# More dummy products of ones in jobs 1 and 2 of a one-core attention and feed-forward kernel

## Chip, cores, metric

The kernel runs on one core of a Trainium2 chip. The metric is the time of one execution on the device in microseconds; of several executions the median is taken. A core has five engines that run their own instruction streams side by side: PE (TensorE, matrix products; its weight loads are shown apart as PEld), DVE (VectorE), ACT (ScalarE), POOL (GpSimd) and SP (SyncE, which here issues the transfers). Each engine works through its own stream in a fixed order, and waits on semaphores that other engines and transfers raise.

## What is computed

Causal attention with a bias for 4 batches of 8 heads (576 positions, 64 columns per head), then two feed-forward layers on the joined heads. Cut to what matters:

```python
def _attn_ref(q, k, v, s):
    scores = scale * np.matmul(q, k.transpose(0, 1, 3, 2))
    cum = np.cumsum(np.maximum(s, 0.0), axis=-1)
    bias = -(cum[:, :, :, None] - cum[:, :, None, :])
    scores = np.where(causal, -1000000000.0, scores + np.minimum(bias, 0.0))
    attn = np.exp(scores - np.max(scores, axis=-1, keepdims=True))
    attn = attn / (np.sum(attn, axis=-1, keepdims=True) + 1e-09)
    return np.matmul(attn, v)
def _moe_ref(x, mu_k, mu_r, w_k, w_v, w_r):   # x_prev is x shifted by one position
    xk = mu_k * x + (1.0 - mu_k) * x_prev
    xr = mu_r * x + (1.0 - mu_r) * x_prev
    k = np.maximum(xk @ w_k, 0.0)
    return sigmoid(xr @ w_r) * (k * k @ w_v)
# a second feed-forward layer (_moe2_ref) with a norm and a gate over positions follows
```

The change touches nothing of this: it adds products whose results are never read.

## The kernel before, in words

Attention is cut into jobs, one job a pair of heads and some blocks of rows. For the first batch each pair makes two jobs: jobs 0 to 3 hold the row blocks 0, 1 and 2 of the four pairs, jobs 4 to 7 the blocks 3 and 4. A job of the first four has five score steps. A score step (`scores`, lines 366 to 411) is a product of queries and keys into a PSUM bank (line 366, full float32), a fold with the mask and the row minimum on DVE (line 381), an exponential on ACT (line 408), and then some **dummy products**: a 128 x 384 product of bfloat16 ones into the bank named `warm` (line 411), whose result nobody reads. How many stand behind each score step of job n is `WD[n]` (line 42), and jobs from the fifth on have none. Each dummy is tied by `behind` to the score product just issued: a tie of order alone, without a semaphore. In `rows` a job turns its probabilities with PE transposes (line 445) into two banks, ACT copies a bank (line 449), and products with the values follow (lines 451 and 455). Behind the transposes of a bank stand `WT[n]` dummies (lines 447 and 448). The first block of rows has its own small chain: line 463 on POOL, a transpose (465), a copy on ACT (467), products (471) and copies (472), and the job ends with a transpose (483) and a copy on ACT (484).

While jobs 0 to 7 run, weights come in. SP issues the loads of queries, keys, the bias row and values of the coming jobs (`load`, lines 203 to 220) and of the weights' words (`load_words`, line 100), all on one queue, in one order; `fetch` calls for the operands of the next job or two, which can only be written once the job before the last has read its own. Each piece of a weight is then taken apart by ACT and DVE (`assemble` and `convert`, lines 111 to 115, 72 and 75): the first step of each conversion is an ACT instruction (line 111) that needs the words to have landed. ACT runs these between the exponentials and copies of the jobs, in its one order.

`step(att, PA)` and `step(cvs, PC)` give the instructions of attention and of the conversions their priorities (-1000 and -500, a lower figure first), and the planner puts every engine's stream into a fixed order ahead of the run by a timeline of its own (`schedule_with_timeline_sim=True`). PE starts with 22 dummies (line 264) while the first operands are loaded. From about 60 us on the first feed-forward layer (line 690) runs beside the attention of the later jobs, then the second layer. The bank `warm` comes out of the pool of two banks that the feed-forward products use; it is given up after the last dummy of job 3.

```python
WD = (2, 1, 1, 2)
WT = (2, 1)
...
            for _ in range(WD[w.n] if w.n < len(WD) else 0):
                behind(nc.tensor.matmul(idle[:, 0:384], ones[:, 0:P], ones, start=True, stop=True), issued[0])
...
            for _ in range(WT[w.n] if w.n < len(WT) else 0):
                behind(nc.tensor.matmul(idle[:, 0:384], ones[:, 0:P], ones, start=True, stop=True), issued[0])
            nc.scalar.copy(tiles[tag][:, o : o + 512], bank)
```

Of the kernel before, what the change touches and what calls it, by code (L numbers as in the profile page):

```python
# [38 lines left out]
NS, NV = 8, 8  # L39
PACE = 3  # L40

WD = (2, 1, 1, 2)
WT = (2, 1)
GT = 150
N0 = 8
ENG0 = {"qh": "DA", "ql": "P", "kh": "A", "kl": "D", "vh": "DA", "vl": "P"}
# [7 lines left out]
def block_kernel(ctx: ExitStack, tc: tile.TileContext, qkv, vb, s, w_r, w_k, w_v, mu, w_in, w_out, w_sgT, g_ln, b_sg, out):  # L54
# [105 lines left out]
    def behind(i, j):  # L160

        kind = mybir.DependencyInfo(mybir.DependencyClass.NoSync, mybir.DependencyReason.DATA)
        tc.add_manual_dep(i.ins, j.ins.name, kind)
# [207 lines left out]
    def scores(w):  # L371
# [13 lines left out]
        for j, i in w.steps[0] + w.steps[1]:  # L385
# [23 lines left out]
            exps.append(i)  # L409
            for _ in range(WD[w.n] if w.n < len(WD) else 0):  # L410
                behind(nc.tensor.matmul(idle[:, 0:384], ones[:, 0:P], ones, start=True, stop=True), issued[0])
# [8 lines left out]
    def rows(w):  # L420
# [15 lines left out]
        for tag, o, pieces, ready in plan:  # L436
# [3 lines left out]
            for x, (i, j, c) in enumerate(pieces):  # L440
# [5 lines left out]
                at[i, j, c] = tiles[tag][:, o + x * P : o + (x + 1) * P]  # L446
            for _ in range(WT[w.n] if w.n < len(WT) else 0):
                behind(nc.tensor.matmul(idle[:, 0:384], ones[:, 0:P], ones, start=True, stop=True), issued[0])
# [749 lines left out]
```

## Time and profile before

| what | value |
|---|---|
| median of 3 runs | 676.12 us (674.73 to 676.29) |
| the profiled execution's own time | 676.66 us |
| its span, first to last instruction | 674.8 us |
| outside the span | 1.86 us |
| PE busy | 653.7 us, 97% of the span |
| DVE, ACT, POOL busy | 519.8, 426.1, 46.2 us |
| mean granted clock of TensorE | 0.997 of full speed |

The profile is that of one execution, 0.54 us above the median of the runs. The span is what the trace covers. Times in the trace count from its start, in microseconds. A PE row's duration includes the drain of the last product, so two rows that follow each other closely overlap by a fraction of a microsecond; the distance of their starts is what PE spent. What follows "idle before" names the engine, tile and line that ended a wait.

### The profile page before, as it was taken

What the parts mean: (1) busy time and instruction counts of PE and PEld (TensorE: products, weight loads), DVE (VectorE), ACT (ScalarE), POOL (GpSimd) and SP (SyncE); (2) the same over time, 40 slices, a digit from 0 to 9 for tenths busy, and PEclk for the clock granted to TensorE, in tenths of its full rate; (3) what the DMA queues carried; (4) which work ended last, traced back from release to release, by engine and by line L of the source; (5) the groups of instructions that cost most, each with busy time, mean ns of one, the idle gap of its engine ahead of it and who ended that gap; (6) DMA issues with size and microseconds to landing.
All of it is one profiled execution on the core that took longest, in us unless ns stands there. A gap on an engine that the chain in (4) does not pass through costs nothing.

```text
span 674.8 us, 12820 instructions
## 1 busy us (share of the span) xinstructions
PE 653.7 (97%) x4590; PEld 612.4 (91%) x4590; DVE 519.8 (77%) x1329; ACT 426.1 (63%) x1014; POOL 46.2 (7%) x95
## 2 busy tenths in 40 slices
PE   7898999899999999999999999999999999999998
PEld 4666989798889999999999999999998998998997
DVE  7798867988889997878996659727488786867856
ACT  6788977779768977958986849526354423233222
POOL 6010000011100100100110100000000000000002
PEclk9899999999999999999999999999999999999999
DMA  7899332353433234233211074103131150320222
GB/s 202 256 271 273 111 96 82 102 161 94 112 109 118 84 87 130 80 94 120 79 44 65 11 262 146 54 36 125 53 123 36 53 160 1 106 71 0 89 80 71
DMA packets 41399, 71.65 MB, mean 106 GB/s; under 512 B 8244, under 2 KB 23968, under 8 KB 41304
## 3 DMA queue, kind: packets, MB, share of 16 engines
q1 hardware_dynamic: 41336, 70.84, 34.9%
q8 instruction: 36, 0.59, 0.4%
q14 instruction: 27, 0.22, 0.1%
HBM read 56.29 MB, written 10.19 MB: 99 GB/s over the span
## 4 chain that ended last, share of the span: by engine, by line
PE 78%; DVE 7%; DMA 5%; ACT 5%; issue 2%; POOL 1%; SPq 1%; DVEq 0%; ACTq 0%; POOLq 0%
PE m L690 30%; PE pu L703 8%; PE ps L1000 4%; PE av L539 3%; PE p L1000 3%; PE t L554 3%; PE pg L963 3%; PE pg L964 2%; PE pg L962 2%; PE av L455 2%; PE pv L894 2%; PE pv L893 2%; PE pv L892 2%; PE s L366 2%; PE s L369 2%
## 5 line engine op out<-in xcount | busy, mean ns | idle before, releaser
L408 ACT ACTIVATE pr<-pr,nm 128x448 f32<-128x448 f32 (+4 forms) x144 | 84.9, 592 | 18.3 <-DVE nm L381 17.9
L690 PE MATMUL m<-xh,wk 128*128 128x288 f32 x512 | 85.8, 301 | 0.3 <-ACT kf L650 0.3
L690 PE MATMUL m<-kh,wv 128*128 128x288 f32 x512 | 79.4, 297 | 0.0
L690 PEld LDWEIGHTS m<-xh,wk 128*128 128x128 f32 x512 | 73.2, 189 | 2.9 <-ACT kf L650 0.8
L381 DVE CUSTOM_DVE_ANT_0 pr<-s,mask 128x320 f32<-128x320 f32 (+3 forms) x128 | 60.6, 476 | 18.9 <-PE s L369 11.5
L690 PEld LDWEIGHTS m<-kh,wv 128*128 128x128 f32 x512 | 71.6, 188 | 0.5
L75 DVE TENSOR_TENSOR xl<-xf,xh 128x288 fp32r<-128x288 f32 (+1 forms) x80 | 40.7, 524 | 12.0 <-ACT xh L828 8.8
L690 PE MATMUL m<-xl,wk 128*128 128x288 f32 x256 | 47.7, 299 | 0.0
L557 ACT CAST pth<-t 128x512 fp32r<-128x512 f32 (+1 forms) x72 | 37.9, 533 | 14.1 <-PE t L554 13.3
L558 DVE TENSOR_TENSOR ptl<-t,pth 128x512 fp32r<-128x512 f32 (+1 forms) x72 | 43.6, 612 | 3.8 <-ACT pth L557 3.5
L368 PE MATMUL s<-qk 128*128 128x288 f32 (+4 forms) x132 | 42.0, 320 | 2.1 <-DVE nh L381 1.0
L690 PE MATMUL m<-kl,wv 128*128 128x288 f32 x256 | 43.7, 298 | 0.0
L622 ACT ACTIVATE xf<-xt,mu 128x288 f32<-128x288 f32 x64 | 33.1, 535 | 15.0 <-POOL xt L520 10.3
L690 PE MATMUL m<-xh,wr 128*128 128x288 f32 x256 | 41.8, 300 | 0.0
L554 PE MATMUL t<-early,pr 128*128 128x128 f32 x252 | 39.0, 273 | 2.6 <-DVE ptl L558 2.6
L369 PE MATMUL s<-qk 68*128 68x288 f32 (+4 forms) x132 | 40.2, 309 | 0.3 <-DMA qk<-gate_d 0.3
L628 DVE SCALAR_TENSOR_TENSOR xf<-xt,mu_sb,xf 128x288 f32<-128x288 f32 x64 | 32.3, 513 | 9.4 <-ACT xf L622 9.1
L703 PE MATMUL pu<-xh,wi 128*128 128x288 f32 x256 | 39.4, 295 | 0.0
L690 PEld LDWEIGHTS m<-xl,wk 128*128 128x128 f32 x256 | 38.7, 188 | 0.6 <-issue 0.2
L650 ACT ACTIVATE kf<-m 128x288 f32<-128x288 f32 x64 | 26.2, 412 | 19.3 <-PE m L690 18.8
L963 PE MATMUL pg<-wg,vh 128*128 128x288 f32 x128 | 37.8, 295 | 0.0
L690 PEld LDWEIGHTS m<-kl,wv 128*128 128x128 f32 x256 | 37.4, 189 | 0.4
(284 smaller groups left out, 1711.9 us busy)
## 6 DMA issues: line engine op xcount, KB each, us to landing
qld<-qkv SPq DMA_DIRECT2D x24, 288.0 KB
kld<-qkv SPq DMA_DIRECT2D x24, 288.0 KB
x_d<-rt SPq DMA_DIRECT2D x8, 576.0 KB
xf<-x_d SPq DMA_DIRECT2D x8, 576.0 KB
vld<-qkv SPq DMA_DIRECT2D x24, 160.0 KB
qk<-qk SPq DMA_DIRECT2D x24, 144.0 KB
ot<-x_d SPq DMA_DIRECT2D x24, 144.0 KB
outT<-ot SPq DMA_DIRECT2D x24, 144.0 KB
```

Of the source, the lines that this page charges most:

```text
L75: (nc.gpsimd if pick(engines) == "P" else nc.vector).tensor_tensor(dst, a, b.bitcast(F32), ALU.subtract)
L368: nc.tensor.matmul(dst, qk[0][:, 0, qs], qk[0][:, 1, ks], start=True, stop=False)
L369: issued[0] = nc.tensor.matmul(dst, qk[1][0 : D + 4, 0, qs], qk[1][0 : D + 4, 1, ks], start=False, stop=True)
L381: nc.vector.tensor_tensor_reduce(out=dst, in0=src, in1=msk, scale=-0.125, scalar=first, op0=ALU.add, op1=ALU.min, accum_out=acc)
L408: i = nc.scalar.activation(dst, dst, AF.Exp, bias=nm[:, col : col + 1], scale=-1.0, accum_out=acc)
L554: issued[0] = nc.tensor.transpose(bank[:, o : o + P], x, ident)
L557: nc.scalar.copy(pth[:, cols], bank[:, 0:o])
L558: nc.vector.tensor_tensor(ptl[:, cols], bank[:, 0:o], pth[:, cols].bitcast(F32), ALU.subtract)
L690: i = nc.tensor.matmul(dst, w(x, c, m), xx[:, c], start=(n + c == 0), stop=(n == 2 and c == w.nk - 1))
L703: nc.tensor.matmul(dst, w(x, c, m), xx[:, c], start=(n + c == 0), stop=(n == 2 and c == w.nk - 1))
L963: nc.tensor.matmul(pg[:, 0:HD], vh[k][:, ds], wg[1][k][:, hs], start=False, stop=False)
L1000: nc.tensor.matmul(dst, wq[a][:, y, c, ms], x[z][c], start=(n == 0), stop=(n % 6 == 5), skip_group_check=(n >= 6))
```

## The change

Two tuples of numbers are changed. Behind each of the five score steps of a job stand two dummies in job 0 (as before), three in job 1 (one before), two in job 2 (one before) and two in job 3 (as before). Behind each of the two transpose banks stand two dummies in job 0 (as before) and two in job 1 (one before). That is 5 x 2 + 2 x 1 = 12 more dummies in job 1 and 5 x 1 = 5 more in job 2, 17 in all; no other instruction is added, moved or removed by the text of the kernel.

```diff
-WD = (2, 1, 1, 2)
-WT = (2, 1)
+WD = (2, 3, 2, 2)
+WT = (2, 2)
```

## Rows read from the trace of the kernel before

**Rows 1.** The page, part 2: granted clock of TensorE in 40 slices, tenths of full speed.

```profile
PEclk9899999999999999999999999999999999999999
```

**Rows 2.** The chain of waits, 0 to 80 us: start, duration, what.

```profile
20.10 0.38 PE t L471 x2
20.47 0.27 SPq L203
...
21.59 5.12 DMA wk11w<-w_k
...
26.80 0.66 ACT cvt L111
27.45 0.48 ACT p L449
...
46.27 7.73 DMA wv10w<-w_v
...
59.09 0.49 PE av L451 x2
```

**Rows 3.** Line 411: duration min/median/max in ns, first and last start.

```profile
L411 PE MATMUL warm<-early x30: 326/326/527, 7.2 to 41.8; 128*128 128x384 bf16 x30
```

**Rows 4.** PE's timeline, 12 to 41 us: start, duration, line, tile, shape, count, wait.

```profile
13.36 1.10 PE L366 MATMUL s<-qk 128*128 128x320 f32 x4 [1.46 <-POOL qk L168]
...
15.82 0.49 PE L411 MATMUL warm<-early 128*128 128x384 bf16 x2
...
16.96 0.49 PE L366 MATMUL s<-qk 128*128 128x128 f32 x2 [0.54 <-DVE nm L381]
17.28 0.33 PE L411 MATMUL warm<-early 128*128 128x384 bf16 x1
17.44 0.39 PE L451 MATMUL av<-vb,p 128*128 128x130 f32 x2
...
19.77 0.33 PE L411 MATMUL warm<-early 128*128 128x384 bf16 x1
...
25.13 0.33 PE L411 MATMUL warm<-early 128*128 128x384 bf16 x1
27.98 0.49 PE L451 MATMUL av<-vb,p 128*128 128x130 f32 x2 [2.53 <-ACT p L449]
...
31.86 0.53 PE L411 MATMUL warm<-early 128*128 128x384 bf16 x1
32.18 0.54 PE L366 MATMUL s<-qk 128*128 128x192 f32 x2
...
38.07 0.39 PE L451 MATMUL av<-vb,p 128*128 128x130 f32 x2
...
40.40 0.49 PE L411 MATMUL warm<-early 128*128 128x384 bf16 x2
```

**Rows 5.** Stretches around the gap: busy PE, PEld, DVE, ACT, POOL; PEclk, DMA share, GB/s.

```profile
25.46:27.98 2.52, 0.00 (x0) 0.00 (x0) 0.49 (x2) 1.19 (x3) 0.00 (x0) 1.00 0.90 278
27.98:28.93 0.95, 0.95 (x8) 0.95 (x9) 0.59 (x3) 0.95 (x3) 0.00 (x0) 0.96 0.90 250
28.93:32.30 3.37, 3.37 (x14) 2.79 (x14) 1.74 (x6) 2.26 (x7) 0.22 (x1) 0.50 1.00 309
```

**Rows 6.** Waits of SP's queue, 0 to 62 us: waiter, waited for, total, times, longest.

```profile
SPq L203 <- DMA wk01w<-w_k: 2.1, 1, 2.1
...
SPq L203 <- PE t L471: 0.4, 1, 0.4
...
SPq L203 <- DMA wr20w<-w_r: 1.8, 1, 1.8
...
SPq L203 <- PE t L445: 0.4, 1, 0.4
```

**Rows 7.** Transfers while SP waits: the stretch of 21 to 22 us, columns as in rows 5.

```profile
21.00:22.00 1.00, 1.00 (x5) 0.53 (x6) 1.00 (x3) 0.81 (x3) 0.00 (x0) 1.00 0.35 65
```

**Rows 8.** SP's timeline: start, duration, line, transfer, count.

```profile
24.83 0.36 SPq L100 DMA_DIRECT2D wk21w<-w_k  x1
```

## Prediction

> **What bounds the kernel now.** I read the page first: over the whole span PE is the bound, and its granted clock is under nine tenths in one of 40 slices only, the second (17 to 34 us) [rows 1]. The dummies of line 411 lie between 7.2 and 41.8 us [rows 3], those of line 448 among them, so the change is decided in the start, before PE becomes nearly gapless at about 59 us. For the start I read the chain of waits [rows 2]. The reader is to see that it isn't a chain of PE alone: PE releases a load on SP at 20.47, behind which SP issues the words of weight piece wk11 at 21.59; they land 5.12 us later; ACT's conversion, first in its order, starts at 26.80, and only behind it the copy that PE wants, so PE resumes at 27.98. Later the same happens once more: wv10 is issued at 46.27, takes 7.73 us, and ACT's stream behind it releases PE at 59.09. PE's timeline shows the first of the two as a gap of 2.53 us [rows 4], and the stretches show what comes of it [rows 5]: the clock, full through the gap, falls to half (1.2 of 2.4 GHz) at about 28.93, 0.95 us after PE resumed, and is back at about 32.3. An idle of 1.46 us at 12 us was followed by no such fall [rows 4].
>
> **What is added, and its price.** By counting off five steps per job, job 1's dummies of line 411 begin with the pair at 15.82 (its first two steps) and the singles at 17.28 and 19.77; job 2's end with the singles at 25.13, 31.86 and 32.56 [rows 4]. Beside them stand the new ones: 4 at 15.82, 2 at 17.28, 2 at 19.77, 6 between 22 and 25 us (job 1's last step and its two banks, job 2's first two steps), 1 at 25.13, and 2 behind the gap, at about 32 us. A single that is followed at once took 0.16 us from its start to the next start (17.28 to 17.44), and a pair shows 0.49 against 0.33 for one, again 0.16 [rows 4]. At half clock it is 0.32 (31.86 to 32.18). So 17 x 0.163 = 2.8 us of PE, of which 15 x 0.163 = 2.45 us stand ahead of the gap.
>
> The Trainium skill, "TensorE: Matmul & The Clock Gate", section "Back-to-back issue gap", gives a sustained distance in streams of weight loads and products that is as small as 131 ns for products of 512 columns; with it as an estimate from above for these 384 columns the 17 would cost at most 2.2 us. The rows show 0.16 us, more than that, and the sum goes by the rows.
>
> **Where they lie.** The four at 15.82 (0.65 us) stand in front of a wait of 0.54 us for DVE's fold [rows 4]; 0.1 us of them is left over. The two at 17.28 and the two at 19.77 have no such cover: PE runs without a hole from 16.96 to the transposes and products of 20.1, so line 471 comes 0.1 + 4 x 0.163 = 0.75 us later. That is where SP hangs: its load of job 3's operands had waited 2.1 us for a transfer and then 0.4 us with PE's line 471 as the last to come [rows 6]. If PE is truly the last, SP and all that is queued on it moves by up to 0.75 us; if the transfer is, by nothing, since the releaser is inferred. The chain's row names PE too [rows 2], so I take 0.6, nearer to that end. Queued behind that load are two bias rows and the words of wk11, wk21, wk31 and wr00. The transfer engines were mostly idle then, a share of 0.35 from 21 to 22 us [rows 7], so a later issue is a later landing: wk11 at 27.3 instead of 26.7, PE's release at 28.6 instead of 27.98.
>
> PE itself reaches the gap at 25.46 + 2.45 - 0.54 (the covered wait), less some 0.1 in small holes, about 27.25. So the gap shrinks from 2.53 to about 1.35 us. It hides 1.8 us of the added work, and it is now below the 1.46 us that brought no fall. I take it that the clock stays full. What that gives back is a comparison of like with like: from the first value product to the dummy behind the next 320-column score took 2.33 us in job 1 (17.44 to 19.77) and in job 3 (38.07 to 40.40), but 3.88 us in job 2 (27.98 to 31.86) [rows 4]. That is 1.55 us, and 0.16 more for the dummy at 31.86 that ran at half rate. With 0.32 for the two new dummies there, PE stands at 33 us by 0.6 - 1.55 - 0.16 + 0.32 = 0.8 us **earlier** than before, though it has done 2.8 us more work.
>
> **What of that reaches the end.** Little, since the next long wait is not PE's. From 21.6 to 42 us SP is held by transfers: a later load of queries and keys waited 1.8 us for wr20's words [rows 6], and these come 0 to 0.6 us later. The only late place where PE's head start helps SP is the load that waits 0.4 us for line 445 [rows 6], so the gain there is at most 0.4 us. Then SP issues the words of wv00 and wv10 back to back, and ACT's release of PE at 59.09 hangs on wv10's landing [rows 2]; PE's early arrival in between only lengthens its wait for ACT. So the release at 59.09 moves by between -0.4 and +0.75 us; I take +0.3, half of the 0.6 by which the transfers start later. From there PE is nearly gapless, its work the same, and the end moves with its start. If the cover at 28 us were gone, the 1.8 us hidden there would be added to this.
>
> Every dummy is tied by order alone, so no wait is added and nothing is queued behind one. The bank that they write is given up after the last dummy of job 3, as before, so the feed-forward products, which share its pool, get it no later than PE's own shift.
>
> The sum against the profiled execution: 676.66 + 0.3 = 676.96 us. That execution lies 0.54 us above the median of the runs; carried over to the median the forecast is **676.4 us**. A measurement of this kernel can tell a change of 0.3% (2.0 us) from none, so this is no change.
>
> **Rivals.** (a) The clock falls all the same, because a gap of 1.35 us and the thin work on either side of it suffice here too: the fall came 0.95 us after PE was busy again [rows 5]. Then PE is 0.6 + 0.16 + 0.32 = 1.1 us later at 33 us, and this time late enough to hold SP's load behind line 445; the end moves by up to 1.1 us: 677.2, still within 0.3%. Chance 0.15.
>
> (b) Slower: the planner's order on ACT. ACT's stream is fixed by a timeline in which PE now has 2.45 us more to do before 25 us, while conversions have the lower priority and fill ACT whenever a copy isn't ready. In the trace the copy of job 1's second bank already stands behind one conversion, at 26.80 [rows 2]. If it moves behind one more whose words land later (wk21's are issued at 24.83 [rows 8], 3.2 us behind wk11's), PE's gap grows by 3.2 us, the clock falls too, and PE is 1.1 + 3.2 = 4.3 us late at 33 us. With the head room of some 0.8 us elsewhere in the start this is 3.5 us at the end, near 679.6. It decides from the point at which the planner has ACT free before the delayed transposes; against it speaks that the next conversion needs a temporary that the one before the last must first give up. Chance 0.2, its range 678.2 to 680.
>
> (c) Faster: the same planner puts that copy ahead of the conversion that waits for wk11. Then PE doesn't wait for the transfer at all: a further 2.4 us on top of the 0.8, at most 3.2 us, and as much reaches the end as the loads behind it move too: 672.9 to 674.0, say 673.4. For it speaks that every added dummy also shifts conversions that follow PE's copies; against it that the copy becomes ready later, not earlier, in the planner's timeline. Chance 0.2.
>
> (d) The change doesn't do what it says, in that the dummies all land where PE waits anyway, or the load on SP follows the transfer and not PE: then SP doesn't move, PE is 1.4 us early at 33 us, and the end moves by -0.4 to 0: 675.9. It lies inside the forecast's range.
>
> **Numbers.** The forecast with (d) has 0.45 (675.7 to 676.9) and (a) 0.15, so within 0.3% holds 0.6; (c) is faster by over 0.3% with 0.2, (b) slower with 0.2. The range of 8 in 10 reaches to the middle of (c) and of (b): 673.2 to 679.3. All 17 on the path and none hidden would be 676.1 + 2.8 = 678.9, inside it.
>
> **What would show it.** Right: 45 dummies of line 411 and 8 of line 448; PE's gap ahead of line 451 at about 28 us near 1.35 us and its release near 28.6; the granted clock full from 25 to 35 us; wk11 issued at about 22.2; the dummies behind job 2's fourth score near 30.9 instead of 31.86; wv10's words landing within 0.7 us of 54.0. Wrong: half clock between 25 and 35 us (a); another instruction between or ahead of line 111 and line 449 on ACT at 27 us (b or c); a release at 59 us that moved by more than 1.2 us, or a PE after 60 us whose waits differ from before's, since I take that stretch as unchanged.

## The result and the profile after

| | before | after |
|---|---|---|
| median of 12 runs | 675.45 us (672.31 to 676.29) | 678.35 us (676.04 to 681.36) |
| ratio | | 1.0052, 95% interval 1.0034 to 1.0071 |
| the profiled execution's own time, span | 676.66, 674.8 us | 679.76, 678.0 us |

The change makes the kernel slower by 0.5%, 2.9 us in the medians. The forecast was a median of 676.4 us, 0.3 us more than the 676.12 then known, called no change. The time lies inside the range given, on the side that rival (b) stood for. The two profiled executions lie above the medians of their kernels, by 1.2 and 1.4 us.

The page of after, the busy line and the line of granted clocks (tenths, 40 slices of 17 us):

```profile
PE 656.6 (97%) x4607; PEld 614.9 (91%) x4607; DVE 519.1 (77%) x1329; ACT 426.7 (63%) x1014; POOL 46.2 (7%) x95
PEclk9999999999999999999999999999999999999999
```

PE has 17 instructions more than before and 2.9 us more busy time (656.6 against 653.7), which is about 17 x 0.163. Read alone this would suggest that the added products are the cost. They are not, as e1 and e2 below show. PE's timeline in after (start, busy us, line, operation, count, and in brackets the idle time before it with what ended it), which answers to [rows 4]:

```profile
15.82 1.14 PE L411 MATMUL warm<-early 128*128 128x384 bf16 x6
16.80 0.27 PE L465 MATMUL t<-early,pr 128*128 128x128 f32 x1
16.94 0.49 PE L366 MATMUL s<-qk 128*128 128x128 f32 x2
...
25.31 0.81 PE L411 MATMUL warm<-early 128*128 128x384 bf16 x4
29.08 0.30 PE L465 MATMUL t<-early,pr 128*128 128x128 f32 x1 [2.96 <-ACT p L449]
29.99 0.49 PE L451 MATMUL av<-vb,p 128*128 128x130 f32 x2 [0.61 <-ACT p L449]
...
31.41 0.74 PE L451 MATMUL av<-vb,p 128*128 128x130 f32 x2
...
32.69 0.74 PE L366 MATMUL s<-qk 128*128 128x128 f32 x2
...
40.25 0.49 PE L366 MATMUL s<-qk 128*128 128x128 f32 x2 [0.59 <-DVE nm L381]
...
41.88 0.39 PE L451 MATMUL av<-vb,p 128*128 128x130 f32 x2
```

Six dummies at 15.82 take 1.14 us, and the score product behind them waits for nothing any more: that cover was real. But the gap at 28 us didn't shrink: 2.96 and 0.61 us in place of 2.53. The value products at 31.41 take 0.74 us where the same two at 18.82 took 0.44: half clock once more, and the stretch from 30 to 40 us has a granted clock of 0.83 (the row stands further down). Job 2's first value product starts at 41.88 instead of 38.07 [rows 4]. (The value products at 17.44, 27.98 and 38.07 of before belong to jobs 0, 1 and 2, whose transposes stand ahead of them; the prediction names these places by the job whose score steps run beside them.)

The chain of waits of after (start, us, what), the lines that answer to [rows 2]:

```profile
21.07 0.30 SPq L203
...
22.22 5.08 DMA wk11w<-w_k
...
27.38 0.66 ACT cvt L111
28.04 0.42 ACT xf L622
28.46 0.47 ACT p L449
28.93 0.52 ACT wk L72
29.45 0.49 ACT p L449
29.95 0.04 issue
29.99 0.49 PE av L451 x2
```

In before one copy stood behind the conversion of wk11 (line 111), at 27.45 [rows 2], and the copy of the first bank had been done ahead of it (ACT's timeline of before):

```profile
23.39 0.59 ACT L449 COPY p<-t 128x512 f32<-128x512 f32 x1
```

Here **both** copies of line 449 stand behind it, and line 622 and a cast of line 72 stand between. The planner gave every engine but POOL another order: the streams of before and after differ from about 18 us on (ACT, DVE), 20 us on (PE) and 22 us on (SP), to 136 us on SP and to about 150 us on the others, and are the same from there but for nine places of DVE at 512 to 521 us. For instance job 2's third score step, ahead of the gap in before, stands behind job 1's value products in after, at 32.69. In before (PE's timeline):

```profile
24.80 0.49 PE L366 MATMUL s<-qk 128*128 128x128 f32 x2
```

### The profile page after: what moved, and what is told of

Its sections match the earlier page's. It is cut to its first block, busy times and chain, and to the rows that moved or that the text cites. A ratio compares the mean times of both kernels' runs of the same rounds, so it can differ in the third digit from the quotient of the medians.

```text
span 678.0 us, 12860 instructions
## 1 busy us (share of the span) xinstructions
PE 656.6 (97%) x4607; PEld 614.9 (91%) x4607; DVE 519.1 (77%) x1329; ACT 426.7 (63%) x1014; POOL 46.2 (7%) x95
## 4 chain that ended last, share of the span: by engine, by line
PE 81%; DVE 7%; ACT 5%; DMA 3%; issue 2%; POOL 1%; SPq 0%; DVEq 0%; POOLq 0%; ACTq 0%
PE m L690 32%; PE pu L703 8%; PE ps L1000 4%; PE av L539 3%; PE t L554 3%; PE p L1000 3%; PE av L455 3%; PE pg L963 3%; PE pg L964 2%; PE pg L962 2%; PE s L366 2%; PE pv L894 2%; PE pv L892 2%; PE pv L893 2%; PE s L369 2%
```

## Experiments

The planner can be taken out of the question. A kernel may plan the program twice: once with the dummy counts `WD_ORDER, WT_ORDER`, to record each engine's order of all instructions but the dummies, and a second time with the counts `WD, WT` that are wanted, each stream tied to the recorded order by ties of order alone (cut to what matters, with names shortened, here and in the edits below):

```diff
+WD_ORDER, WT_ORDER = (2, 1, 1, 2), (2, 1)     # whose order
+WD, WT = (2, 3, 2, 2), (2, 2)                 # whose dummies (here e1)
+    def follow(tc, traced, order):
+        for engine, ran in order.items():
+            for a, b in zip(ran, ran[1:]):
+                tc.add_manual_dep(traced[b], traced[a].name, NoSync)
```

Theory A of the quoted texts is that the planner's order is the cost, theory B that PE's added work is.

**e1: after's dummies in before's order.** The edit above.

> All 53 dummies of the changed kernel, but every engine's stream tied to the order of the kernel before (the dummies slip in behind their products). Theory A (the planner's new order is the cost): the time is that of before within 1 us, as the forecast's sum says (about +0.3 us); PE's gap ahead of line 451 is 1.35 us, its release near 28.6, and the clock stays full. Theory B (the added 2.8 us of PE work is the cost): the time is 2.4 to 3.2 us above before.

Measured: 674.62 us, ratio 0.9999 (0.9978 to 1.0021). The 17 products cost nothing that can be measured within 0.2%. The order was held: in e1's trace ACT, DVE, SP and PE without its dummies run before's instructions one by one. Of the gap theory A has the release right and its length wrong:

```profile
28.53 0.78 PE L451 MATMUL av<-vb,p 128*128 128x130 f32 x2 [1.95 <-ACT p L449]
```

The release is at 28.53 (28.6 expected), but the gap is 1.95 us and not 1.35, and the clock falls to half behind it.

**e2: before's dummies in after's order.** The two pairs of counts exchanged.

> The 36 dummies of the kernel before, but every engine's stream tied to the order of the changed kernel. Theory A: at least 2 us above before, since the order is the cost; the gap ahead of the value products is there and longer than before's 2.53 us. Theory B: the time of before within 0.8 us.

Measured: 678.15 us, ratio 1.0047 (1.0027 to 1.0066). Without one added product the order costs all but 0.05% of what the change costs, and in e2's trace the four streams are those of after, one by one. The gap is there and longer than before's 2.53 us (PE's timeline of e2):

```profile
27.99 0.45 PE L465 MATMUL t<-early,pr 128*128 128x128 f32 x1 [2.84 <-ACT p L449]
28.91 0.80 PE L451 MATMUL av<-vb,p 128*128 128x130 f32 x2 [0.47 <-ACT p L449]
```

Of the cost, theory A holds and theory B falls.

**e3: before, with wk11's conversion behind the copies.** Which part of the order is it? The first suspect is the wait at 28 us. On ACT line 111 of wk11 is moved behind the copies and exponentials that PE wants, on DVE its next two steps (lines 114 and 115). The numbers are places in the traced program; 215 is line 111 of wk11, 216 and 217 are its lines 114 and 115:

```diff
+    for engine, what, behind in (("Activation", 215, 275), ("DVE", 216, 425), ("DVE", 217, 216)):
+        ran = order[engine]
+        ran.remove(what)
+        ran.insert(ran.index(behind) + 1, what)
```

> The kernel before in its own order, but for one thing: the first step of wk11's conversion on ACT (line 111) and its two on DVE (lines 114 and 115) stand behind the copy, the exponentials and the cast that followed them. If the gap at 25.5 us is made by that one instruction's wait for the transfer, the gap shrinks from 2.53 us to under 0.5, the clock stays full, and PE is 2.5 to 4 us earlier at 38 us. If the start is held by PE and its predecessors up to 59 us, 2 to 3 us of that reach the end (faster by 0.3 to 0.5%); if the later transfers hold it, as the forecast had it, at most 0.5 us do.

Measured: 674.05 us, ratio 0.9979 (0.9956 to 1.0001). PE's timeline in its profile has no gap at 28 us, and job 1's value products run at 24.70:

```profile
24.54 0.33 PE L411 MATMUL warm<-early 128*128 128x384 bf16 x1
24.70 0.39 PE L451 MATMUL av<-vb,p 128*128 128x130 f32 x2
24.92 1.00 PE L455 MATMUL av<-vb,p 128*128 128x65 f32 x8
```

The gap is gone and 3.3 us are won at this place (27.98 to 24.70), but the median lies only 1.4 us below before's, with an interval that just reaches no change.

**e4: the same with after's dummies.**

> As the run before (old order, wk11's conversion behind), with the dummies of the changed kernel. Without the gap nothing hides the 2.8 us of added products. Theory B in its strict form (PE is the bound in the start): 2.4 to 3 us above the run with the old dummies. Forecast's view (transfers and ACT hold the end of the start): within 1 us of it.

Measured: 674.86 us, ratio 0.9995 (0.9974 to 1.0015). That is 0.8 us above e3, where theory B in its strict form had 2.4 to 3; the forecast's view, within 1 us, holds.

**e5: after, with the conversion put back behind the copies**, the rest of the new order kept (ACT: lines 111 and 72, DVE: lines 114, 115 and 75 of wk11; 218 and 219 are lines 72 and 75).

```diff
+    for engine, what, behind in (("Activation", 215, 260), ("Activation", 218, 253), ("DVE", 216, 274), ("DVE", 217, 216), ("DVE", 219, 254)):
+        ...
```

> The changed kernel with its dummies and its own new order, but for one thing: the first steps of wk11's conversion (line 111 on ACT, lines 114 and 115 on DVE, and the cast and difference behind them) stand behind the copies and exponentials of job 2's start, which the new order had put behind them. Theory A1 (the new order costs because this one conversion, which waits for its transfer, stands ahead of two copies that PE needs): the gap of 2.96 and 0.61 us ahead of the value products shrinks below 1 us and the time falls by 2 to 4 us, to within 1 us of the kernel before. Theory A2 (the cost is spread over many exchanges in the first 110 us, such as scores of job 2 moved behind value products): it stays 2 us or more above before.

Measured: 677.13 us, ratio 1.0017 (0.9998 to 1.0037). The gap is gone, but behind it PE now waits 1.19, 0.41 and 0.56 us, and then the clock falls (two rows of PE's timeline of e5):

```profile
26.24 0.41 PE L451 MATMUL av<-vb,p 128*128 128x130 f32 x2
...
33.87 1.43 PE L366 MATMUL s<-qk 128*128 128x320 f32 x2 [0.56 <-DVE nm L381]
```

The time is 1.8 us above the median of before that was measured beside it (675.34) and 1.2 below after's: it falls between theories A1 and A2.

**e6: before, with the conversion ahead of both copies**, as the new order has it.

```diff
+    for engine, what, behind in (("Activation", 215, 192), ("DVE", 216, 199), ("DVE", 217, 423)):
+        ...
```

> The kernel before with its dummies and its order, but for the same conversion of wk11, moved ahead to where the new order has it: ahead of both copies and the mixing step on ACT, ahead of two folds on DVE. Theory A1: 1.5 to 3.5 us above before, with a gap at 25.5 us longer than 2.53 us by about the time of two more ACT instructions (1 us). Theory A2: within 0.8 us of before.

Measured: 677.2 us, ratio 1.0014 (0.999 to 1.0038), with the longer gap in its profile:

```profile
28.27 0.45 PE L465 MATMUL t<-early,pr 128*128 128x128 f32 x1 [3.77 <-ACT p L449]
```

Spoiling the one place in the old order isn't told from before by this, and mending it in the new order takes back a part of the cost: neither carries all of it.

**e7 and e8: both kernels profiled once more**, unchanged, to see which differences of the two traces come again.

> The kernel before, unchanged, for a second profile. If the fall of the clock at 29 us belongs to the kernel, it is there again, at the same place and for the same 3.4 us; if it hangs on the execution, the gap of 2.53 us is there without it, or the fall lies elsewhere.

> The changed kernel, unchanged, for a second profile. The gap ahead of the value products near 28 to 30 us is there again with its two copies behind the conversion of wk11 (about 3.5 us in sum); the fall of the clock behind it is there again if a gap of that length is enough in every execution.

Measured: 676.09 and 677.91 us, one execution each. In e7 the gap is 2.30 us, in e8 it is 1.62 and 0.61, and the clock falls behind it in both. PE's timeline of e8, where two dummies at 30.65 take 0.85 us for 0.49 at full clock:

```profile
25.03 0.81 PE L411 MATMUL warm<-early 128*128 128x384 bf16 x4
27.46 0.30 PE L465 MATMUL t<-early,pr 128*128 128x128 f32 x1 [1.62 <-ACT p L449]
28.37 0.49 PE L451 MATMUL av<-vb,p 128*128 128x130 f32 x2 [0.61 <-ACT p L449]
...
30.65 0.85 PE L411 MATMUL warm<-early 128*128 128x384 bf16 x2
```

wk11 was issued at 20.9 us here and at 22.2 in the first profile, so this gap differs by over 1 us between executions of one kernel. Where PE stood, as the start of its products, in both executions of each kernel:

| us | before | e7 | after | e8 |
|---|---|---|---|---|
| line 451, job 1 | 27.98 | 27.18 | 29.99 | 28.37 |
| line 451, job 2 | 38.07 | 37.27 | 41.88 | 40.23 |
| line 451, job 7 (last) | 102.55 | 101.45 | 104.18 | 102.50 |
| line 495, first (job 8) | 120.45 | 119.35 | 122.08 | 120.41 |
| line 892, first | 416.6 | 416.0 | 419.7 | 417.8 |

After is late by 3.4 us at job 2 and by 1.3 at job 7, each as the mean of two executions; single executions of one kernel lie 0.8 to 1.7 us apart here. From job 8 to the first product of line 892 after needs 297.6 and 297.4 us, before 296.1 and 296.65 (one clock fall of 1.7 us lies in the last, at 192 us). All profiles bear this stretch out: with the falls in it taken off at 1.7 us each it takes 296.2 to 297.6 us in the four with the whole new order (after, e8, e2, e5; mean 297.0) and 294.5 to 296.4 in the eight with the old order on ACT, DVE and PE (mean 295.1), wk11's conversion apart. Behind that every profile of this document takes the same 258.3 us to the end of its span. So the cost has two places, the start and the stretch behind 120 us, and the second, 1.9 us, is the more firmly shown. There PE's waits in after are these among others (its timeline):

```profile
136.31 0.52 PE L554 MATMUL t<-early,pr 128*128 128x128 f32 x3 [0.83 <-DVE ptl L558]
152.83 0.44 PE L539 MATMUL av<-pth,vv 128*128 128x384 f32 x1 [1.16 <-ACT pth L557]
171.55 0.80 PE L690 MATMUL m<-xh,wr 128*128 128x288 f32 x4 [0.45 <-ACT kf L650]
```

In before the first of them is 0.16 us, and the other two don't show:

```profile
134.97 0.52 PE L554 MATMUL t<-early,pr 128*128 128x128 f32 x3 [0.16 <-DVE ptl L558]
```

The first belongs to the order: it is 0.83 or 0.84 us in all four profiles with the new order, and 0.16 or 0.17 in all eight with the old one. The other two come again in e8, at 0.57 and 0.48 us, but not in e2, which has before's dummies.

**e9, e10, e11: after's order on some engines only**, before's on the others, before's dummies throughout. In e9 ACT and DVE take the new order, in e10 PE, in e11 SP:

```diff
+    WD, WT = WD_OTHER, WT_OTHER
+    other = plan()[1]
+    for engine in ("Activation", "DVE"):       # e10: ("PE",)   e11: ("SP",)
+        order[engine] = other[engine]
```

> The kernel before with its own dummies; ACT and DVE run in the order of the kernel after, PE and SP in the order of before. The whole new order cost 0.47% (e2, 678.15 against 675.46). If the order of the conversions on ACT and DVE is the cost (theory A), this run takes all of it, 1.0047, about 678.5 us, with PE's gap at 28 us above 2.6 us. If the order of the loads on SP is the cost, through later words of weights (rival S), this run shows 1.000, 675.4 us. If PE's own order is the cost (rival P), 1.000 too. If the three only cost together (rival T), under 1.0015.

> The kernel before with its own dummies; PE runs in the order of the kernel after, ACT, DVE and SP in the order of before. Theory A (conversions on ACT and DVE): 1.000, 675.4 us. Rival S (loads on SP): 1.000. Rival P (PE's own order, in which job 2's last score step stands behind its value products): 1.0047, 678.5 us. Rival T (only together): under 1.0015.

> The kernel before with its own dummies; SP runs in the order of the kernel after, ACT, DVE and PE in the order of before. Theory A (conversions on ACT and DVE): 1.000, 675.4 us. Rival S (loads on SP, the queries and keys behind the words of further weights): 1.0047, 678.5 us, with the landing of wv10's words or of the queries behind them more than 1 us later than in before. Rival P: 1.000. Rival T (only together): under 1.0015.

Measured: e9 687.05 us, 1.0181 (1.015 to 1.0212); e10 687.61 us, 1.0155 (1.0116 to 1.0193); e11 675.6 us, 1.0002 (0.9983 to 1.0021). SP's order alone is not the cost: rival S falls. For the other two no theory had foreseen this: each half of the new order costs more than three times as much as the whole (e2, 0.47%). PE's waits from 10 to 110 us come to 14.4 and 14.7 us in e9 and e10, against 8.0 in before and 8.4 in e2. The costliest (us in total, times, longest), in e9:

```profile
PE t L471 <- ACT xt L472: 4.1, 3, 1.8
PE t L465 <- ACT p L449: 3.4, 2, 2.5
PE s L366 <- DVE nm L381: 2.6, 4, 0.7
```

and in e10:

```profile
PE t L483 <- DVE avt L480: 3.3, 2, 2.2
PE s L366 <- DVE nm L381: 2.8, 5, 0.9
PE m L690 <- ACT kf L650: 2.4, 1, 2.4
```

That ACT's and DVE's order fits PE's of the same plan, and that a stream out of step with the others waits, is the reading of these rows. So the new order's cost can't be shared out between PE on the one side and ACT and DVE on the other.

**e12: e3 again**, with more rounds.

> The kernel of e3 once more: before, with the first steps of wk11's conversion moved behind the copies and exponentials that PE wants at 28 us. e3 measured 0.9979 with an interval from 0.9956 to 1.0001. If the wait for wk11's words costs at the end what the gap shows at 28 us (2.5 us and the clock's fall behind it), 0.9965 or less, 673 us. If e3's gain was the spread between executions alone, 1.000, 675.4 us. Between the two, 0.998, if the released time is taken back in part by later waits for wv00's and wv10's words.

Measured: 675.1 us, ratio 0.9991 (0.997 to 1.0013). With e3 that is 22 executions whose mean, 674.49, lies 1.0 us (standard error 0.5), 0.14%, below the mean of before's 80. No version here is clearly shown to beat before; the gain is between nothing and 0.3%.

**What the clock does in all of them.** Each execution comes with its mean granted clock. In the stretches of 10 us of all profiles, up to line 892, the loss comes in multiples of 1.7 us: a stretch at 0.83, or two that lose as much together (or twice as much), as one fall of 3.4 us at half clock would [rows 5]. The profile of after has one such fall behind the gap, e1's has three, two of them behind the gap (stretch, its length and the busy time of PE, PEld, DVE, ACT and POOL, the granted clock, the DMA share, GB/s). After:

```profile
30.00:40.00 10.00, 9.66 (x50) 7.21 (x50) 7.57 (x25) 7.44 (x20) 1.31 (x2) 0.83 1.01 325
```

e1:

```profile
20.00:30.00 10.00, 8.05 (x48) 5.83 (x47) 6.95 (x23) 6.52 (x17) 0.88 (x1) 0.93 0.84 234
30.00:40.00 10.00, 9.30 (x44) 6.59 (x44) 5.58 (x18) 5.88 (x15) 1.12 (x2) 0.73 0.94 282
130.00:140.00 10.00, 9.59 (x57) 8.46 (x55) 7.50 (x22) 5.68 (x15) 0.25 (x1) 0.83 0.33 90
```

Its execution of 679.41 us has a mean clock of 0.992, e3's without a fall 1.000. So an estimate of what an execution lost to the clock is its time x (1 - mean clock), and of its time at full clock the rest. The estimate is rough. Among the 80 executions of before one microsecond lost goes with 0.72 us of time (standard error 0.06), not with 1; and in eight of the fourteen profiles 0.2 to 0.65 us of the loss lies behind line 892, where the time doesn't differ. The means, with the standard error in brackets:

| kernel | runs | time | mean clock | lost to clock | rest |
|---|---|---|---|---|---|
| before | 80 | 675.45 | 0.9945 | 3.7 (0.2) | 671.7 (0.1) |
| e1: dummies new, order old | 12 | 675.24 | 0.9967 | 2.3 (0.6) | 673.0 (0.2) |
| e2: dummies old, order new | 12 | 678.25 | 0.9930 | 4.7 (0.4) | 673.5 (0.5) |
| after: both new | 12 | 678.40 | 0.9949 | 3.4 (0.4) | 675.0 (0.4) |
| e6: before, spoiled | 11 | 676.48 | 0.9928 | 4.9 (0.6) | 671.6 (0.1) |
| e3 and e12: before, moved behind | 22 | 674.49 | 0.9962 | 2.6 (0.4) | 671.9 (0.2) |
| e4: e3 with new dummies | 10 | 674.77 | 0.9972 | 1.9 (0.5) | 672.9 (0.4) |
| e5: after, repaired | 12 | 676.97 | 0.9967 | 2.3 (0.4) | 674.7 (0.3) |

The parts add up. By this split the dummies cost 1.3 us of rest (e1) and save 1.4 us of clock, in the new order too (after against e2: 1.3 us saved). The new order costs 1.8 us of rest and 1.0 of clock (e2). Both together: 3.1 us of rest by the sum, 3.2 measured. Where wk11's conversion stands hardly touches the rest (e6, e3 and e5 against before and after: -0.1, +0.2, -0.2); what it moves is the clock's part, by +1.2, -1.2 and -1.2 us. The differences of the clock's part have standard errors of 0.4 to 0.6 us, so each of them is about two to three errors from nothing, and how much of a loss reaches the end is a matter of the split.

## Why the prediction was right in its range and wrong in its path

The range holds the measured time because it reaches to the middle of rival (b). The forecast itself, a change of +0.3 us, is not what was measured: +2.9 us, with an interval that leaves no change out.

**The step that failed** is the one that takes ACT's order as given: "wk11 at 27.3 instead of 26.7, PE's release at 28.6 instead of 27.98" carries before's order over to after. The landing was right (27.30), the release was 29.99, since both copies now stand behind the conversion. From the start of line 111 to job 1's first value product it is 1.19 us in before, e7 and e1, and 2.6 us in after, e8 and e2: 1.4 us that belong to the order. The prediction did name the planner, as rivals (b) and (c), with 0.2 each, and priced one exchange on ACT. What e1 and e2 show is that the change of order is the whole effect that can be measured, and that it is not one exchange but four streams over 130 us. Mending the one exchange (e5) takes back 1.4 us (standard error 0.5) of the 2.9, by the split hardly any of it at full clock.

**Rival (b)** has the sign and the maker, not the mechanism. wk21's conversion doesn't stand ahead of the copy; wk11's does, as in before, and takes the first bank's copy along. The price, 3.5 us, is near the 2.9 measured by luck: its terms, a wait for wk21's words and a gap longer by 3.2 us, aren't there. **Rival (c)**, PE no longer waiting for wk11, was priced at 673.4, 2.7 us below the median then known. e3 and e12 make that exchange by hand with before's dummies and lie 1.0 us (standard error 0.5) below before, e4 makes it with the new ones and lies 0.7 us (0.6) below. Of the 2.4 us that the wait seemed to be worth 1 us or less reaches the end.

**The price of the dummies** was right: 6 of them take 1.14 us, so (1.14 - 0.33) / 5 = 0.16 us each. This is the rows' 0.16 and not the 131 ns for 512 columns of the Trainium skill's "TensorE: Matmul & The Clock Gate", section "Back-to-back issue gap". Of 2.8 us 1.3 us reaches the rest by the split (e1), so 1.5 us is hidden, against 1.8 by the prediction. But what stands ahead of the gap was mis-sized: with the order held PE reached it at 26.58 (28.53 - 1.95) and not at 27.25, so that more than the 0.1 us taken for small holes was absorbed on the way, and the gap stayed at 1.95 us.

**SP's load that hangs on PE**: wk11 was issued at 22.2 us in after, as forecast, and at 22.4 in e1's profile. But it was 20.9 in e8, 21.1 in e4 and 21.9 in e5, and with before's dummies 21.2 to 21.8 in eight profiles and 22.6 in e10. A shift of 0.6 us is no larger than the spread of single executions, so it is neither shown nor refuted. Two readings beside it don't hold. Two rows of [rows 6], those of lines 471 and 445, are of shorter windows than its heading says. From 0 to 62 us SP's waits in before begin with

```profile
SPq L203 <- PE t L471: 4.0, 2, 3.7
```

so the longest wait between 21.6 and 42 us, 3.7 us ahead of the load issued at 32.75, ended with PE, where the prediction says that SP is held by transfers there. And "nothing is queued behind" a dummy is not what the trace of after shows: over the same 0 to 62 us a load of SP waited last for one, as far as the profile can infer who came last:

```profile
SPq L203 <- PE warm L411: 2.2, 1, 2.2
```

What either of these costs at the end no run here tells.

**The clock stays full** was wrong. Gaps of 2.96 and of 1.62 with 0.61 us (after, e8) and of 1.95 us (e1) were each followed by a fall, and so were the 1.19, 0.41 and 0.56 us of e5. This step took one idle of 1.46 us without a fall for a bound. Still, a gain near the 1.7 us that it was priced at is there as a mean, 1.4 us (0.6) over twelve executions of e1, and the net forecast for the dummies alone (+0.3) agrees with e1 (675.24 against 675.45, a difference of -0.2 with a standard error of 0.6). That agreement is in part luck, since neither the gap nor the clock of e1's profile is as forecast.

**The time after 60 us as unchanged** was wrong: before's order and after's differ up to 150 us, and from 120 us to line 892 the new order costs 1.9 us at full clock, 0.7 of it the wait ahead of line 554 (0.83 against 0.16 us).

**wv10's words** were expected within 0.7 us of 54.0; in after they were issued at 43.4 instead of 46.3 and hold nobody. PE's products of line 451 at 59.09 come at 62.11, and the new order has put sixteen products of line 690 (59.87 to 62.11) ahead of them.

What stays open: which of the exchanged steps make up the 1.8 us of rest beyond the wait ahead of line 554, and why more than half of the loss at job 2 is regained by 102 us. The mixed orders (e9, e10) can't tell, since each of them costs more than the whole.

## What to carry to other kernels

Where a planner fixes every engine's order, a filler instruction that waits for nothing can still change the plan: compare the orders of the two programs before weighing microseconds, and measure the edit once with the old order held. A gap that is mended at one place need not be paid out at the end (3.3 us won at 28 us in e3, 1 us or less of it in the mean): judge by many executions, and look at the mean granted clock of each beside its time.

## What was unexpected of the hardware

The spread between executions of one kernel, 672 to 680 us in the 80 of before, goes in good part with a count of clock falls, each 3.4 us at half clock and 1.7 us lost: 0 in e3's profile (mean clock 1.000, 671.56 us), 1 in after's, 2 in e7's, 3 in e1's (0.992, 679.41 us). Before has about two of them in the mean of 80 executions (3.7 / 1.7). About two thirds of the variance of before's times go with the loss, and with the loss taken off their standard deviation falls from 1.5 to 1.0 us.

The falls come at the gap of 28 us, but also near 131 and 192 us, there too behind a wait of PE, at 129.53 in e1 and at 190.94 in e7:

```profile
129.53 0.47 PE L368 MATMUL s<-qk 128*128 128x448 f32 x1 [1.04 <-DVE nh L381]
190.94 0.52 PE L554 MATMUL t<-early,pr 128*128 128x128 f32 x3 [1.62 <-DVE ptl L558]
```

That PE is busy in 9.59 of the 10 us from 130 on in e1 doesn't speak against it: products that run at half clock count as busy for longer. The wait of 1.04 us stands in before, e7, after, e8 and e2 as well (1.03 to 1.05), and no fall came behind it there, nor behind the 1.46 us at 12 us [rows 4]. So in these traces the length of one wait doesn't tell whether a fall follows; it differs between executions of one program.
